# Sharing two-bank PSUM tiles between block products in the last group's first layer

## The chip, the cores and the metric

The kernel runs on one core of a Trainium2 chip. The metric is the device time in microseconds of one launch; the kernel before took 513.73 us (median of 3 runs, 512.77 to 514.19). A core has TensorE (PE, matrix products, written into PSUM), VectorE (DVE), ScalarE (ACT), GpSimd (POOL), and SyncE (SP), which issues DMAs. PSUM has eight banks; each holds 512 fp32 numbers in each of 128 partitions. The engines run their own instruction queues in order and wait for one another by semaphores.

## The reference

Two blocks follow each other. The first is a delta-rule attention over 4 batches, 8 heads, 768 tokens and a head dimension of 48:

```
k_n = k / (norm(k) + 1e-6)
for t in range(S):
    y[t] = q[t] @ state
    v_old = state^T k_n[t]
    state += beta[t] * outer(k_n[t], v[t] - v_old)
```

The result is laid out as x with 3072 rows (tokens) of 384 columns, and goes through a feed-forward block whose hidden layer is the maximum of three products:

```
h = max(x @ w1, x @ w2, x @ w3)      # w1, w2, w3: 384 x 768
out = h @ w_out                      # 768 x 384
```

## The kernel before, in words

The tokens are worked in six groups of 512. The attention of later groups is interleaved with the feed-forward part (`ffn`, a generator) of earlier ones, in an order written out by hand; a framework records which instruction writes and reads each tile and places the semaphore waits. When the last group's feed-forward part starts there is no attention work left, so from there to the end the kernel is one chain of layers.

From the second group on, the first product is taken out of the maximum: the kernel holds the differences w2-w1 and w3-w1 and computes h = max(0, x(w2-w1), x(w3-w1)), and x·w1·w_out is added in the output layer. In the code the differences are `w_sb[1]` and `w_sb[2]`.

For the last group the hidden layer is `crossed_hidden` (L1067). It splits the tokens into two halves of 256 (`lo`, `hi`) and the 768 hidden columns into two halves of three blocks of 128, and forms the four blocks of such a 2x2 product from seven products of sums and differences in place of eight. That covers the first two of x's three row blocks of 128; the third is added directly (`c1`, `c2`). A *unit* is one block pair j (three of them) and one difference matrix i (two), six in all. A unit makes eight block products, numbered 0 to 7, each 128 x 256 in fp32, with 1, 2, 1, 1, 1, 2, 2 and 1 matmuls (L1102), so 11 a unit:

- products 0, 2, 3 and 4 are copied to SBUF by ScalarE (L1121, L1127, L1130, L1134) as m1, m7, m5, m6;
- after product 4 VectorE adds these up in four steps (L1135 to L1138);
- products 1, 5, 6 and 7 are each read by VectorE (L1108), which adds them to a base in SBUF; in units with i = 1 a second VectorE instruction (L1110) takes the maximum with the hidden value of i = 0.

Four sums of the input halves (s1 to s4, L1083 to L1086) are made by VectorE ahead of the first unit.

A product's place in PSUM comes from `bank(n)` (L1114). Two rings exist for the whole kernel and fill the eight banks: `ps_ffn` (L80), one-bank tiles in 2 buffers, and `ps_two` (L83), two-bank tiles in 3 buffers. In the kernel before, even products take the first bank of a `ps_two` tile, whose second bank stays unused, and odd ones a `ps_ffn` tile. A buffer that is handed out again is written only once the readers of its previous content are done.

After the six units `outputs` (L947) runs the last layer, also as a 2x2 product, with two `ps_ffn` tiles p and q (L955) that its matmuls (L960) fill by turns. The same function runs for the group before, directly ahead of `crossed_hidden`; its last store is issued in part by ScalarE's queue (L1043, L981).

Of the kernel before, what the change touches and what calls it, by code (L numbers as in the profile page):

```python
# [23 lines left out]
def kernel(  # L24
# [42 lines left out]
    TOK = 512  # L67
# [12 lines left out]
    def ps_ffn(shape, name):  # L80
        return psum.tile(shape, FP32, name=name, tag="ffn", bufs=2)

    def ps_two(name):  # L83
        return psum.tile([128, 2, 512], FP32, name=name, tag="two", bufs=3)
# [222 lines left out]
    def square(name):  # L307
        return work.tile([128, H, C], FP32, name=name, tag="square", bufs=17)
# [758 lines left out]
    def crossed_hidden(m, hs):  # L1067


        xt, vec = xts[m], nc.vector.tensor_tensor  # L1070
        plus = vec if m == GROUPS - 1 else nc.gpsimd.tensor_tensor
        lo, hi = slice(0, 256), slice(256, 512)
        a11, a12, a13 = (xt[:, t, lo] for t in range(KT))
        a21, a22, a23 = (xt[:, t, hi] for t in range(KT))
        spare = [t.rearrange("p a h d -> p (a h d)") for t in kmore]
        s1, s2, s3, s4 = (spare[0][:, 256 * n : 256 * (n + 1)] for n in range(4))
        parts = [
            work.tile([128, 2, HB * BL + HB], FP32, name=name, bufs=1).rearrange(
                "p s r -> p (s r)"
            )  # L1080
            for name in ("x_bl", "y_bl")
        ]
        vec(out=s3, in0=a11, in1=a21, op=ALU.subtract)  # L1083
        vec(out=s1, in0=a21, in1=a22, op=ALU.add)
        vec(out=s2, in0=s1, in1=a11, op=ALU.subtract)
        vec(out=s4, in0=a12, in1=s2, op=ALU.subtract)  # L1086
        for j in range(FT):
            hs[j] = square("h").rearrange("p h c -> p (h c)")
        for unit in range(2 * PAIRS):
            j, i = divmod(unit, 2)  # L1090
            w = {
                name: t[:, 128 * j : 128 * (j + 1)]
                for name, t in thirds[1 + i].items()
            }
            top, bottom = hs[j], hs[j + PAIRS]
            held = parts[unit % 2]
            m1, m5, m6, m7 = (held[:, 256 * n : 256 * (n + 1)] for n in range(4))
            c11 = spare[1][:, 256 * (unit // 2 % 2) :][:, 0:256]

            def times(to, *terms):  # L1100
                for n, (stays, moves) in enumerate(terms):
                    nc.tensor.matmul(  # L1102
                        to, w[stays], moves, start=(n == 0), stop=(n == len(terms) - 1)
                    )

            def result(h, base, p, spare=None):
                to = h if i == 0 else base if spare is None else spare
                vec(out=to, in0=base, in1=p, op=ALU.add)  # L1108
                if i:
                    nc.vector.scalar_tensor_tensor(  # L1110
                        out=h, in0=h, scalar=0.0, in1=to, op0=ALU.max, op1=ALU.max
                    )

            def bank(n):  # L1114
                return (ps_ffn([128, TOK], "p_e") if n % 2 else ps_two("p_c")[:, 0])[
                    :, 0:256
                ]

            p = bank(0)
            times(p, ("b11", a11))  # L1120
            nc.scalar.copy(m1, p)  # L1121
            p = bank(1)
            times(p, ("b21", a12), ("c1", a13))
            result(top[:, lo], m1, p, c11)
            p = bank(2)
            times(p, ("t3", s3))
            nc.scalar.copy(m7, p)  # L1127
            p = bank(3)
            times(p, ("t1", s1))
            nc.scalar.copy(m5, p)  # L1130
            yield
            p = bank(4)
            times(p, ("t2", s2))
            nc.scalar.copy(m6, p)  # L1134
            plus(out=m6, in0=m6, in1=m1, op=ALU.add)  # L1135
            plus(out=m1, in0=m6, in1=m5, op=ALU.add)
            plus(out=m7, in0=m7, in1=m6, op=ALU.add)
            plus(out=m5, in0=m5, in1=m7, op=ALU.add)  # L1138
            p = bank(5)
            times(p, ("c2", a13), ("b22", s4))  # L1140
            result(bottom[:, lo], m1, p)
            p = bank(6)
            times(p, ("t4", a22), ("c1", a23))
            result(top[:, hi], m7, p)
            p = bank(7)
            times(p, ("c2", a23))
            result(bottom[:, hi], m5, p)
            yield

    def ffn(m):  # L1150
# [32 lines left out]
        if m >= GROUPS - 1:  # L1183
            yield from crossed_hidden(m, hs)
            early = FT
# [288 lines left out]
```

## Time and profile before

| | |
|---|---|
| median of 3 runs | 513.73 us (512.77 to 514.19) |
| span of the profiled execution | 510.5 us |
| its own time | not taken apart; the median of the runs is 3.2 us over the span |
| PE busy | 491.1 us, 96% of the span |
| DVE, ACT, POOL busy | 349.9, 168.7, 192.7 us |
| first matmul of `crossed_hidden` | 454.06 us |
| first L960 matmul of the last output layer | 484.60 us |
| between them: PE busy, DVE busy, ACT busy | 30.16, 23.11, 8.94 us of 30.54 |

The profile is one execution of the program, with the start and length of every instruction. PE is the matmul side of TensorE and PEld its weight loads; an fp32 matmul of this kernel leaves two records on each. A matmul's record reaches from its start to the end of its results, so that records of successive matmuls overlap, and the distance between starts tells what one costs. "Idle before, releaser" is the time in which an engine did nothing ahead of an instruction, and what ended it. Times in views are microseconds from the start of the span, durations in lists with slashes are nanoseconds.

### The profile page before, as it was taken

The numbers are of one execution on the slowest core, as the hardware profiler recorded it, in microseconds if no ns is written. First come the engines' busy times: TensorE is split into PE (matmuls) and PEld (weight loads), VectorE is DVE, ScalarE is ACT, GpSimd is POOL, SyncE is SP. The second block draws the span as 40 slices with busy tenths as digits, with TensorE's granted clock in tenths as the row PEclk, the third lists the DMA queues.
The fourth block names the chain that finished last, engine by engine and source line by source line (L and its number), as shares of the span: only waits on it lengthen the run. The fifth ranks groups of instructions, "written<-read, shape, count | busy, mean of one in ns | idle before, by whom it ended". The sixth has DMA issues, their size and how long they took to land.

```text
span 510.5 us, 18528 instructions
## 1 busy us (share of the span) xinstructions
PE 491.1 (96%) x8016; PEld 333.1 (65%) x8016; DVE 349.9 (69%) x801; ACT 168.7 (33%) x320; POOL 192.7 (38%) x317
## 2 busy tenths in 40 slices
PE   7778989999999999999999999999999999999996
PEld 6567778756565565665555565555655556998796
DVE  5897799969996430899563987635897455456752
ACT  5585664884422242210252101252101412113210
POOL 7434372783491926670575770503130000000000
PEclk9755999999999999999999999999999999999999
DMA  8938869764055925353675454923343202230001
GB/s 111 192 64 221 194 151 155 195 199 100 5 148 140 175 46 130 99 143 83 144 136 130 120 137 94 174 37 92 80 116 81 44 3 64 54 71 2 0 17 46
DMA packets 106304, 53.49 MB, mean 105 GB/s; under 512 B 89712, under 2 KB 99984, under 8 KB 106224
## 3 DMA queue, kind: packets, MB, share of 16 engines
q1 hardware_dynamic: 94352, 31.35, 30.4%
q0 software_dynamic: 9472, 20.37, 16.4%
q8 instruction: 63, 1.03, 0.9%
q10 hardware_dynamic: 2400, 0.59, 0.6%
q14 instruction: 17, 0.14, 0.1%
HBM read 39.17 MB, written 13.11 MB: 102 GB/s over the span
## 4 chain that ended last, share of the span: by engine, by line
PE 73%; DVE 14%; DMA 5%; ACT 4%; SPq 2%; issue 2%; POOL 0%; DVEq 0%; ACTq 0%; POOLq 0%
PE p_h L1161 26%; PE p_o L1199 13%; PE p_o L960 9%; PE p_e L1102 3%; DVE tmp L552 3%; PE p_g L406 3%; PE p_c L1102 2%; PE p_m L894 2%; PE p_u L759 2%; DMA kmore<-in_k_dram 2%; PE p_k L731 2%; PE p_y L801 2%; DVE y_bl L556 2%; PE p_s L782 2%; PE p_j L714 1%
## 5 line engine op out<-in xcount | busy, mean ns | idle before, releaser
L1161 PE MATMUL p_h<-xt,w_sb 128*128 128x512 f32 (+1 forms) x450 | 187.5, 558 | 0.7 <-ACT xt L827 0.6
L1161 PEld LDWEIGHTS p_h<-xt,w_sb 128*128 128x128 f32 x450 | 82.3, 193 | 68.7 <-issue 61.8
L1199 PE MATMUL p_o<-wo_sb,h 128*128 128x384 f32 x192 | 65.3, 490 | 0.0
L1175 DVE TENSOR_TENSOR h<-h,p_h 128x512 f32<-128x512 f32 (+1 forms) x42 | 25.4, 606 | 53.9 <-PE p_h L1161 52.8
L552 DVE TENSOR_TENSOR tmp<-x_bl,y_bl 128x31 f32<-128x31 f32 (+20 forms) x139 | 51.3, 369 | 4.1
L556 DVE TENSOR_TENSOR y_bl<-y_bl,tmp 128x31 f32<-128x31 f32 (+20 forms) x139 | 48.5, 349 | 4.8
L1199 PEld LDWEIGHTS p_o<-wo_sb,h 128*128 128x128 f32 x192 | 35.7, 190 | 23.2
L364 POOL DMA_DIRECT2D turned<-in_q_dram x72 | 39.1, 551 | 4.3 <-POOL turned L359 2.9
L1205 ACT COPY o_sb<-p_o 128x384 f32<-128x384 f32 x16 | 7.7, 479 | 85.8 <-PE p_o L1199 79.8
L1171 ACT ACTIVATE h<-p_h 128x512 f32<-128x512 f32 x24 | 14.3, 597 | 63.4 <-PE p_h L1161 60.5
L254 POOL TENSOR_TENSOR w_sb<-mant,up 128x384 int32<-128x384 int32 x18 | 19.1, 1059 | 39.3 <-DVE mant L250 39.2
L406 PEld LDWEIGHTS p_g<-kqt 48*64 48x64 f32 x1216 | 24.6, 142 | 9.0 <-issue 6.4
L406 PE MATMUL p_g<-kqt 48*64 48x64 f32 (+1 forms) x1216 | 27.8, 242 | 0.9 <-ACT kqt L335 0.8
L789 DVE TENSOR_TENSOR st<-st,p_s 48x768 f32<-48x768 f32 (+1 forms) x18 | 17.1, 949 | 15.4 <-PE p_s L782 15.2
L120 POOL DMA_DIRECT2D kpad<-in_k_dram x32 | 21.8, 690 | 14.1 <-issue 12.7
L1199 PE MATMUL p_o<-w_sb,xt 128*128 128x384 f32 x72 | 25.2, 486 | 0.0
L139 POOL DMA_DIRECT2D v_t<-in_v_dram x14 | 11.5, 829 | 35.5 <-PE p_u L759 35.5
L390 DVE TENSOR_TENSOR pt<-p_g,mask 128x512 f32<-128x512 f32 x20 | 13.8, 688 | 15.9 <-PE p_g L406 15.8
L287 POOL TENSOR_TENSOR v_t<-v_t,nrm 128x768 f32<-128x768 f32 x12 | 17.9, 1493 | 9.0 <-DVE nrm L281 8.9
L359 POOL MEMSET turned<- 128x96 f32 x18 | 3.3, 192 | 47.6 <-DVE kqt L380 47.6
L759 PEld LDWEIGHTS p_u<-v_t,ut 64*64 64x64 f32 x768 | 13.4, 141 | 10.1 <-issue 7.8
L1199 PEld LDWEIGHTS p_o<-w_sb,xt 128*128 128x128 f32 x72 | 13.7, 190 | 9.5
(212 smaller groups left out, 837.0 us busy)
## 6 DMA issues: line engine op xcount, KB each, us to landing
out_dram<-o_sb SPq DMA_DIRECT2D x40, 96.0 KB
w_bits<-in_moe_w_dram SPq DMA_DIRECT2D x9, 384.0 KB
w_bits<-in_moe_w_dram POOLq DMA_DIRECT2D x9, 384.0 KB, 5.2
turned<-in_q_dram POOLq DMA_DIRECT2D x72, 48.0 KB, 2.9
kpad<-in_k_dram POOLq DMA_DIRECT2D x32, 96.0 KB, 6.1
y_x<-y SPq DMA_DIRECT2D x16, 192.0 KB
qall<-y_x SPq DMA_DIRECT2D x32, 96.0 KB
v_t<-in_v_dram POOLq DMA_DIRECT2D x14, 192.0 KB, 5.0
```

The lines of the kernel that those rows point to most:

```text
L120: queues[bb].dma_start(out=dst[rows(bb ^ g), :, 0:D], in_=src[2 * bb + g, :, c * C : (c + 1) * C, :].rearrange("h p d -> p h d"),)
L254: nc.gpsimd.tensor_tensor(out=dst.bitcast(I32), in0=mant_v.bitcast(I32), in1=up_v, op=ALU.add)
L364: (queue, nc.gpsimd)[i].dma_start(out=t[p0 : p0 + 32, bb, at : at + NP * 2 * D].rearrange("p (j x) -> p j x", j=NP), in_=(k, q)[i][2 * bb ...
L406: nc.tensor.matmul(p_g[rows(bb ^ (g * i)), par, c0 : c0 + C * (1 + whole)], kq[:, 0], kq if whole else kq[:, i],)
L552: nc.vector.tensor_tensor(out=t_v, in0=row.to_broadcast(t_v.shape), in1=column.to_broadcast(t_v.shape), op=ALU.mult,)
L556: nc.vector.tensor_tensor(out=rest, in0=rest, in1=t_v, op=ALU.subtract)
L759: nc.tensor.matmul(p_v[rows(bb ^ g), g, i], ut[c % NU][rows(bb), g, h], rhs[rows(bb), g, h],)
L960: nc.tensor.matmul(to[:, g], a[j][:, 128 * g : 128 * (g + 1)], b[j], start=(start and g == j == 0), stop=(stop and g == 1 and j == PAIRS - 1),
L1102: nc.tensor.matmul(to, w[stays], moves, start=(n == 0), stop=(n == len(terms) - 1))
L1161: nc.tensor.matmul(p_h, w_sb[i][:, t, f * 128 : (f + 1) * 128], xt[:, t, lo : lo + w], start=(t == 0), stop=(t == KT - 1),)
L1175: nc.vector.tensor_tensor(out=h, in0=h, in1=p_h, op=ALU.max)
L1199: nc.tensor.matmul(p_o, stays, moves, start=(n == 0), stop=(n == len(terms) - 1))
```

## The change

Products 0 to 5 now take the two banks of a `ps_two` tile by pairs: (0,1), (2,3), (4,5), the even one in the first bank and the odd one in the second. Products 6 and 7 take one `ps_ffn` tile each. A unit thus asks for three `ps_two` and two `ps_ffn` tiles where it asked for four and four. The matmuls, copies and sums and their order stay the same. From L1089 on the changed file's lines are one higher, and from L1116 four higher.

```diff
         for j in range(FT):
             hs[j] = square("h").rearrange("p h c -> p (h c)")
+        pair = [None]
         for unit in range(2 * PAIRS):
...
             def bank(n):
-                return (ps_ffn([128, TOK], "p_e") if n % 2 else ps_two("p_c")[:, 0])[
-                    :, 0:256
-                ]
+
+                if n > 5:
+                    return ps_ffn([128, TOK], "p_e")[:, 0:256]
+                if n % 2 == 0:
+                    pair[0] = ps_two("p_c")
+                return pair[0][:, n % 2, 0:256]
```

## The prediction

> **What bounds the kernel now.** I read the page first, for the engine that decides.
>
> ```profile
> span 510.5 us, 18528 instructions
> PE 491.1 (96%) x8016; PEld 333.1 (65%) x8016; DVE 349.9 (69%) x801; ACT 168.7 (33%) x320; POOL 192.7 (38%) x317
> PE   7778989999999999999999999999999999999996
> PEclk9755999999999999999999999999999999999999
> ```
>
> TensorE is busy 96% of the span, so what delays a matmul of the last group lengthens the kernel. Next the windows over the changed stage (first L1102 matmul to the first L960 matmul behind it) and over three early stretches. Columns: stretch, length, busy time and count of PE, PEld, DVE, ACT, POOL, granted clock, DMA share, GB/s.
>
> ```profile
> 12.06:15.48 3.42, 1.77 (x68) 1.46 (x68) 2.85 (x6) 2.07 (x6) 2.19 (x3) 1.00 0.98 169
> 22.30:25.72 3.42, 1.96 (x56) 1.51 (x59) 3.04 (x12) 1.80 (x4) 0.00 (x0) 1.00 1.33 185
> 63.26:66.68 3.42, 2.15 (x70) 1.64 (x69) 3.32 (x8) 2.13 (x5) 0.92 (x2) 1.00 0.37 102
> 454.06:484.60 30.54, 30.16 (x133) 24.23 (x132) 23.11 (x61) 8.94 (x24) 0.00 (x0) 1.00 0.05 14
> ```
>
> In the stage's 30.54 us PE is busy for 30.16 at full clock, ACT for only 8.94. The timeline of the stage gives the prices (start, length, engine, line; in brackets the idle time before and what ended it).
>
> ```profile
> 454.06 0.59 PE L1102 MATMUL p_c<-xt,w_sb 128*128 128x256 f32 x2
> 454.84 0.68 ACTq L981 DMA_DIRECT2D out_dram<-up  x1
> 455.56 0.37 ACT L1121 COPY x_bl<-p_c 128x256 f32<-128x256 f32 x1 [10.52 <-PE p_e L1102]
> 456.32 0.41 DVE L1108 TENSOR_TENSOR h<-x_bl,p_e 128x256 f32<-128x256 f32 x1
> 456.79 0.70 PE L1102 MATMUL p_e<-xt,w_sb 128*128 128x256 f32 x2
> ...
> 460.34 0.59 PE L1102 MATMUL p_c<-kmore,crossed 128*128 128x256 f32 x2
> 460.98 0.37 ACT L1127 COPY y_bl<-p_c 128x256 f32<-128x256 f32 x1 [0.92 <-PE p_c L1102]
> 461.21 0.59 PE L1102 MATMUL p_c<-kmore,crossed 128*128 128x256 f32 x2
> 463.80 0.59 PE L1102 MATMUL p_c<-xt,w_sb 128*128 128x256 f32 x2
> ```
>
> To be seen: one matmul leaves two records and takes 0.432 us of PE (461.21 to 463.80 is six of them, 2.59 us). Its results are there 0.59 us after its start, and ScalarE's copy begins 0.05 later (460.93 to 460.98). The copy lasts 0.37. The last view, from the end of the stage and from an early wait of PE on ScalarE:
>
> ```profile
> 482.14 0.37 ACT L1134 COPY y_bl<-p_c 128x256 f32<-128x256 f32 x1
> 484.60 0.43 PE L960 MATMUL p_o<-wo_sb,h 128*128 128x192 f32 x1 [0.34 <-DVE y_bl L1108]
> ```
>
> ```profile
> L335 ACT COPY kqt<-p_t x2: 586/588/591, 11.8 to 12.3; 128x512 f32<-128x512 f32 x2
> ```
>
> The first L335 copy starts at 11.79, ends at 12.38, and the matmul that waits for it starts at 12.43: 0.05 from the end of a ScalarE copy to PE.
>
> **The change part by part.** Matmuls, copies and VectorE's work keep their number and order; no DMA moves, and no queue (SP, POOL) is passed. What changes is which tile a product is written to, and so which waits stand on the matmuls.
>
> *Removed.* The stage's 66 matmuls (11 a unit) need 66 x 0.432 = 28.5 us, and it lasts 30.54. So 2.0 us are waits now: some 1.5 us on VectorE's readings of the two one-bank buffers within the stage (as the one behind 456.32) and about 0.5 at L960. After the change a product's place comes back a whole unit later, so the waits inside the units go.
>
> *Added.* The order of the built changed program, with its waits, shows the decisive thing: the first matmul of products 1, 3 and 5 of every unit waits for ScalarE, and the count it waits for is that of the copies L1121, L1127 and L1134 of the same unit. Those read the other half of the same pair. Writing the second bank of a tile is thus held until the first bank has been read; before, the two products lay in different tiles. That makes 18 waits. Each stops the whole PE queue, since TensorE takes its matmuls in order, and behind it stand the rest of the unit and the output layer.
>
> The price of one, on PE: 0.59 (even product to its end) + 0.05 (to the copy) + 0.37 (copy) + 0.05 (back to PE) = 1.06 instead of 0.432, so 0.63. After a wait the weights are loaded only then: the pair of records that waited at 456.79 is 0.70 long and not 0.59, so 0.11 more. I take 0.63 + 0.11 = 0.74. Lower bound 0.63 (the load hidden); upper 0.79 (one semaphore instruction of 0.05, as this stage's L1102 row of 51 ns, stands ahead). The value lies with the rows of the stage itself.
>
> *First wait.* ScalarE is busy issuing the last store of the group before (454.84 to 455.52), so the first copy starts at 455.56, as now; before, nobody on PE waited for it. It ends at 455.93, PE resumes at 455.98 and, with the 0.11, at 456.09 instead of 454.49: 1.60.
>
> *Last wait.* The first L960 matmul now reuses the buffer of product 6, freed by VectorE's L1108. In the last unit now VectorE's chain from the L1134 copy's end (482.51) has product 5 read at +2.04 (484.55) and product 6 at +2.83. After the change that copy ends 4.65 into the unit: the five matmuls of products 0 to 3 (2.16) and two waits of 0.74 put product 4's start at 3.64, plus 0.59 + 0.05 + 0.37. Product 6 is read at 7.48, PE resumes at 7.53; the unit's matmuls end at 11 x 0.432 + 3 x 0.74 = 6.97. So 0.56 is left.
>
> *Sum.* 28.5 + 17 x 0.74 + 1.60 + 0.56 = 43.2 us, against 30.54: **+12.7 us**. The output layer behind (484.60 to the end, 25.9 us) only moves: its VectorE inputs get 0.8 us more lead. Costed at nothing: VectorE's work, 23.11 us in a stage of 43; POOL has none there. The profiled execution has a span of 510.5; the median of the runs is 513.73, so 3.2 lie around it. Span 523.2, time 526.4.
>
> *A rule against it.* The row: 1.06 us from an even product's start to the odd one's, because of a wait that the program carries. The Trainium skill, "PSUM — Partial Sum Buffer", section "PSUM bank collisions raise a hardware error", says that two engines collide in one bank and quadrant, while different banks run clean; by it the odd product needs no wait at all, and the sum would be a gain of up to 2 us. No run here shows a collision. I go by the built program.
>
> *The clock.* In the trace it fell to half right behind the two stretches in which PE was busy 1.77 and 1.96 of 3.42 us (15.48 and 25.72), and stayed behind the one of 2.15. In the changed stage gaps of 0.47 us three times in 6.97 leave PE busy 80%, 2.7 of 3.42, above all three. Only the first wait (idle 454.65 to 455.98) with the next one can leave less than 2 us in such a stretch. The skill's page "TensorE: Matmul & The Clock Gate", section "Why this matters for your kernels", asks for idle gaps over some 3 us before the clock falls. The two early stretches have none over 1.5 us, so the trace is stricter; by the page the loss is 0, by the trace up to one half-clock stretch.
>
> **The rivals.**
> 1. *The change does what it says* (the other side): the odd products don't wait, eight products are in flight. Gain 2.0 - 0.5 (last wait stays) = 1.5, time 512.2. It speaks for it that the two halves are used apart; against it the waits named above. It decides if those counts are reached before PE comes there, that is if a copy could end within 0.432 us of its product's start; the rows need 1.01.
> 2. *Clock falls once:* the first wait and the next fall into one stretch. A unit at half clock takes 6.97 + 4.75 = 11.7, so a stretch of 3.41 us loses 1.4: 527.8. If it stayed half for the stage, 28.5 more: 555.
> 3. *Cheaper waits:* 0.63 apiece, 18 x 0.11 less: 524.4. *Dearer:* 0.79, 18 x 0.05 more: 527.3.
>
> **How the numbers follow.** Forecast (0.71 to 0.77 a wait) 0.70; cheaper 0.12, dearer 0.07, one clock stretch 0.06, half clock throughout 0.02, no waits 0.03. The run-to-run spread is 512.77 to 514.19, so no change can be told within 0.3%, 1.5 us. Cheap waits at the fast end of that spread (1.0 below its median) give 523.4; dear ones with one lost clock stretch and the slow end (0.5 above) 529.2. Faster 0.015 and same 0.015 share rival 1, whose gain lies at that border; slower 0.97.
>
> **What would show it.** L1102's matmuls stay at 132 records; 18 PE idle gaps of about 0.47 us ended by ScalarE at L1121, L1127, L1134 (their new lines); units of 7.0 us and a stage of 43; L960's wait on VectorE as now; everything before 454 unchanged. Wrong if PE's waits on ScalarE are absent, if the clock is below 1.00 in the stage, or if the stage before 454 moves.

## The result and the profile after

The changed kernel takes 525.03 us (median of 5 runs, 523.68 to 526.33), the kernel before, in 5 runs, 512.77 (512.18 to 514.19). The ratio is 1.0233, with a 95% interval of 1.0203 to 1.0264: slower by 12 us. The prediction was 526.4, range 523.4 to 529.2.

The page of the changed kernel (the profiled execution took 526.33 us, the slowest of its five, with 1.8 us around the span):

```profile
span 524.5 us, 18530 instructions
PE 493.4 (94%) x8016; PEld 331.3 (63%) x8016; DVE 351.2 (67%) x801; ACT 168.8 (32%) x320; POOL 192.8 (37%) x317
PE   7578989999999999999999999999999999977896
PEclk9855999999999999999999999999999999999999
```

PE's row now has a dent of three slices near the end (7, 7, 8), where it stood at 9 before; the clock has none. The windows over the stage, from the first L1103 matmul (L1102 before) to the first L960 matmul, in the columns used before:

```profile
455.45:498.50 43.05, 33.47 (x135) 23.41 (x133) 24.74 (x63) 8.94 (x24) 0.00 (x0) 1.00 0.04 10
```

43.05 us in place of 30.54, so 12.5 more; behind it to the end of the span it is 26.0 as before (25.9). PE idles for 9.6 us of it, 9.2 ahead of L1103 matmuls and 0.4 ahead of the first L960 one. What ended the idle time is in the view of the line L1103 (microseconds in total, times):

```profile
its engine sat idle before it (us, times) until:
  ACT x_bl L1125: 5.7, 6
  ACT x_bl L1138: 4.0, 6
  ACT y_bl L1138: 4.0, 6
  ACT x_bl L1131: 4.0, 6
  ACT y_bl L1125: 4.0, 6
  ACT y_bl L1131: 4.0, 6
```

L1125, L1131 and L1138 are the copies of products 0, 2 and 4 (L1121, L1127 and L1134 before), and nothing else is in the list. It counts PE's matmuls and weight loads apart, so each gap twice; on the matmul side there are 18 such gaps, one of 1.31 us and 17 of 0.46. Rows of PE and ScalarE from the timeline show the long first gap with the DMA that ScalarE's queue issues, one of the common gaps in the second unit, and the end of the stage:

```profile
456.24 0.65 ACTq L981 DMA_DIRECT2D out_dram<-up  x1
456.93 0.37 ACT L1125 COPY x_bl<-p_c 128x256 f32<-128x256 f32 x1 [10.49 <-DVE kmore L1084]
457.36 1.13 PE L1103 MATMUL p_c<-xt,w_sb 128*128 128x256 f32 x4 [1.31 <-ACT x_bl L1125]
...
463.24 0.59 PE L1103 MATMUL p_c<-xt,w_sb 128*128 128x256 f32 x2
463.87 0.37 ACT L1125 COPY y_bl<-p_c 128x256 f32<-128x256 f32 x1 [2.95 <-PE p_c L1103]
464.29 1.13 PE L1103 MATMUL p_c<-xt,w_sb 128*128 128x256 f32 x4 [0.46 <-ACT y_bl L1125]
470.17 0.59 PE L1103 MATMUL p_c<-xt,w_sb 128*128 128x256 f32 x2
...
498.50 1.73 PE L960 MATMUL p_o<-wo_sb,h 128*128 128x192 f32 x9 [0.41 <-DVE y_bl L1109]
```

In the second unit product 0 starts at 463.24 and is there at 463.83; the copy runs from 463.87 to 464.24; product 1, which goes into the next bank, starts at 464.29. From this product 0 to that of the next unit (470.17) it is 6.93 us.

### The profile page after: what moved, and what is told of

Its sections match the earlier page's. It is cut to its first block, busy times and chain, and to the rows that moved or that the text cites. A ratio compares the mean times of both kernels' runs of the same rounds, so it can differ in the third digit from the quotient of the medians.

```text
span 524.5 us, 18530 instructions
## 1 busy us (share of the span) xinstructions
PE 493.4 (94%) x8016; PEld 331.3 (63%) x8016; DVE 351.2 (67%) x801; ACT 168.8 (32%) x320; POOL 192.8 (37%) x317
## 4 chain that ended last, share of the span: by engine, by line
PE 76%; DVE 12%; ACT 5%; DMA 3%; issue 2%; SPq 2%; POOL 0%; DVEq 0%; ACTq 0%; POOLq 0%
PE p_h L1165 27%; PE p_o L1203 16%; PE p_o L960 8%; PE p_c L1103 5%; PE p_g L406 3%; PE p_m L894 2%; PE p_u L759 2%; DVE tmp L552 2%; PE p_k L731 2%; DMA kmore<-in_k_dram 2%; PE p_s L782 2%; PE p_y L801 2%; PE p_q L731 1%; PE p_j L714 1%; PE p_e L1103 1%
## 5 line engine op out<-in xcount | busy, mean ns | idle before, releaser
L120 POOL DMA_DIRECT2D kpad<-in_k_dram x32 | 21.8, 690 | 13.8 <-issue 12.7
L1103 PE MATMUL p_c<-xt,w_sb 128*128 128x256 f32 x48 | 14.5, 405 | 6.4 <-ACT x_bl L1125 2.2
```

The source lines that it names most:

```text
L120: queues[bb].dma_start(out=dst[rows(bb ^ g), :, 0:D], in_=src[2 * bb + g, :, c * C : (c + 1) * C, :].rearrange("h p d -> p h d"),)
L1103: nc.tensor.matmul(to, w[stays], moves, start=(n == 0), stop=(n == len(terms) - 1))
```

## The experiments

Two theories were set against each other. *The order theory:* a write into one half of a two-bank tile is held until the other half has been read, and the 12.5 us are these waits. *The layout theory:* two banks handed out as one tile, or a copy beside a write into the next bank, are dear by themselves. Stages run from the first matmul of the unit loop to the first L960 matmul of the last layer. Diffs are against the changed kernel. Two baselines matter for what follows: the stage is 30.54 us before and 43.05 as changed. Ratios are to the kernel before.

### The second halves written late

```diff
-        pair = [None]
+        pair = {}
...
-                if n > 5:
+                if n == 0 == unit:
+                    return ps_two("p_c")[:, 0, 0:256]
+                if n < 2:
                     return ps_ffn([128, TOK], "p_e")[:, 0:256]
-                if n % 2 == 0:
-                    pair[0] = ps_two("p_c")
-                return pair[0][:, n % 2, 0:256]
+                if n < 5:
+                    pair[n] = ps_two("p_c")
+                    return pair[n][:, 0, 0:256]
+                return pair[n - 3][:, 1, 0:256]
```

> Products 2, 3 and 4 open the two-bank tiles and 5, 6 and 7 take their second halves; 0 and 1 take the one-bank tiles (product 0 of the first unit takes a two-bank tile of its own). Tiles are still shared, but each second half is written three products after the first, when the first has long been read. Theory (a write to one half is held until the other half has been read): the matmuls that open a second half find the copy done, no PE waits on ScalarE, the stage takes the bare 66 x 0.432 = 28.5 us, 2.0 under the kernel before: 510.8 on a base of 512.8, ratio 0.996. Rival (sharing two banks of a tile is itself dear, whatever the order: the copy's read beside a write into the next bank): 18 products are still written into second halves, so the stage stays near 43 us and the ratio near 1.02.

Ratio 0.9931 (0.9904 to 0.9958), median 510.09 against 513.43. The windows over its stage:

```profile
454.57:483.14 28.57, 28.57 (x133) 24.85 (x133) 22.68 (x59) 8.95 (x24) 0.00 (x0) 1.00 0.06 15
```

PE is busy in all of the 28.57 us: no gap is left. Three products of a unit are still written into second halves, as in the changed kernel, and the stage is 14.5 us shorter. The layout theory falls. The stage's gain over before, 1.97 us, is what the theory said; the ratio asks for more, so the kernel ran again:

> The kernel of late_halves once more. Its stage was 28.58 us against 30.54 before, 1.96 less, but its ratio of 0.9931 asks for 3.5 us. Theory (the rest is the scatter of the part ahead of the stage, which starts at 452.6 to 457.6 in the profiles so far): ratio 0.996, stage 28.6 again. Rival (something outside the stage gains too): ratio 0.993 again.

Ratio 0.9930 (0.9904 to 0.9957), stage 28.58, as long as the first time. So the rival's number came, but no profile shows where the other 1.5 us are: behind the stage the profiles of both kernels show 25.8 to 25.9 us, and ahead of it nothing was changed. It stays open. Either way this kernel is the fastest of all here.

### Both products written, then both read

```diff
             p = bank(0)
             times(p, ("b11", a11))
+            r = bank(1)
+            times(r, ("b21", a12), ("c1", a13))
             nc.scalar.copy(m1, p)
-            p = bank(1)
-            times(p, ("b21", a12), ("c1", a13))
-            result(top[:, lo], m1, p, c11)
+            result(top[:, lo], m1, r, c11)
...
```

(and likewise for products 2 and 3, and 4 and 5)

> The changed kernel's pairs (0,1), (2,3), (4,5), but both products of a pair are written before either is read. Theory (the wait comes from the read standing between the two writes): no PE wait on ScalarE inside pairs; the stage is 28.5 us and the wait ahead of the output layer. If reads are held back by the tile's last write too, product 4's copy starts after product 5's end, 0.86 us later, and the L960 wait grows to some 2.2 us: 30.8, ratio 1.000 to 1.001. If reads look at their own half only: 29.9, ratio 0.999. Rival (the layout is dear): near 43 us, ratio near 1.02.

Ratio 0.9992 (0.9966 to 1.0018), stage 30.68 us: the first of the two sub-cases, 30.8. The end of the last unit in the timeline:

```profile
480.27 0.59 PE L1103 MATMUL p_c<-kmore,w_sb 128*128 128x256 f32 x2
480.90 0.38 ACT L1140 COPY y_bl<-p_c 128x256 f32<-128x256 f32 x1 [0.65 <-PE p_c L1103]
484.17 2.81 PE L960 MATMUL p_o<-wo_sb,h 128*128 128x192 f32 x11 [2.01 <-DVE y_bl L1109]
```

The pairs are the changed kernel's, and all 18 gaps are gone; what was dear is the read between the two writes. The wait works in the other direction too: the copy of product 4 starts at 480.90, 0.04 us behind the last matmul of product 5 (480.86), though product 4 was done earlier. The later copy delays VectorE's sums, and PE's one remaining gap is 2.01 us ahead of the last layer. Behind the stage the profiled execution took 27.6 us in place of 25.9, since the clock fell there for a while (last section); the ratio doesn't show these 1.7 us, and whether the other executions had them no trace tells.

### Eight one-bank tiles

(the diff is shortened)

```diff
+    rings = ctx.enter_context(ExitStack())
+    pools = [rings.enter_context(tc.tile_pool(name="psum", ...))]
...
     def ps_ffn(shape, name):
+        if len(pools) > 1:
+            return pools[1].tile(shape, FP32, name=name, tag="one", bufs=8)
...
             def bank(n):
+                return ps_ffn([128, TOK], "p_e")[:, 0:256]
...
         if m >= GROUPS - 1:
+            rings.close()
+            pools.append(rings.enter_context(tc.tile_pool(name="last", ...)))
             yield from crossed_hidden(m, hs)
```

> For the last group the two rings are given up for one ring of eight one-bank tiles; no tile is shared, and a product's place comes back eight products later, as the change has it. Theory: what the change could have brought without shared tiles. No waits inside the units, none ahead of the output layer, but the first matmul waits for the last reader of the old rings (454.81 in the profile before, so 0.9 us lost): 29.4 us, 1.1 under before, ratio 0.998. Rival (the eight-product distance is of no use): ratio 1.000.

Ratio 0.9980 (0.9957 to 1.0002), as expected for the theory, though the interval does not quite shut out no change. The profile is clearer: 28.59 us from the first matmul with no gap, after the one wait that was expected at the entry:

```profile
457.00 0.56 DVE L994 TENSOR_TENSOR up<-up,p_o 128x384 f32<-128x384 f32 x1 [1.40 <-PE p_o L965]
457.61 1.56 PE L1108 MATMUL p_e<-xt,w_sb 128*128 128x256 f32 x6 [0.65 <-DVE up L994]
```

This is what the change could bring with its reuse distance of eight products and without shared tiles: about 2 us (30.54 against 28.59), of which this form gives 0.8 back at the entry: 0.65 of idle time, and the 0.16 by which a matmul's record otherwise overlaps the one before. That makes the 29.4 us expected.

### Half of the units

```diff
             def bank(n):

+                if unit > 2:
+                    return (ps_ffn([128, TOK], "p_e") if n % 2 else ps_two("p_c")[:, 0])[
+                        :, 0:256
+                    ]
                 if n > 5:
```

> Units 0 to 2 as changed, units 3 to 5 as before. Theory: the loss goes with the number of waits. 7.8 + 2 x 7.0 for the first three units, 15.6 for the last three as in the profile before: 37.4 us, 6.9 over before, ratio 1.013, nine PE waits on ScalarE. Rival (the loss is made at the entry or exit of the stage): ratio 1.023 or 1.000.

The windows over its two halves:

```profile
452.64:474.30 21.66, 16.65 (x68) 11.80 (x67) 12.60 (x32) 4.47 (x12) 0.00 (x0) 1.00 0.08 20
474.30:489.72 15.42, 15.05 (x68) 12.09 (x66) 11.09 (x30) 4.48 (x12) 0.00 (x0) 1.00 0.01 1
```

21.66 us for the units as changed (expected 21.8) and 15.42 for those as before (15.6), with nine waits on ScalarE. The ratio was 1.0088 (1.0054 to 1.0122), less than the stage's 6.5 us ask for. The same kernel ran again:

> The kernel of half_units once more. Its stage was 37.08 us, 6.54 over before, its ratio 1.0088 asks for 4.5. Theory (scatter ahead of the stage): ratio 1.0127, stage 37.1. Rival: 1.009 again.

Ratio 1.0132 (1.0098 to 1.0166), stage 37.07. The loss goes with the number of waits. The two ratios differ by 0.44% at equal stages: the part ahead of the stage scatters (it ended at 452.64 in one of the two profiles and at 453.91 in the other), and a ratio alone can't tell 2 us here.

### Each copy made twice

```diff
             nc.scalar.copy(m1, p)
+            nc.scalar.copy(m1, p)
...
             nc.scalar.copy(m7, p)
+            nc.scalar.copy(m7, p)
...
             nc.scalar.copy(m6, p)
+            nc.scalar.copy(m6, p)
```

> The changed kernel with the copies of products 0, 2 and 4 (m1, m7, m6) made twice, same source and target; the result is the same. Theory (the wait lasts from the even product's end to the end of the last read of its half): each of the 18 waits is longer by one copy and its start, 0.43 us as in the row of two copies following each other; 18 x 0.43 = 7.7 us more than the changed kernel, stage 50.8, ratio to before 1.038. Rival (the price is on PE, in reloading weights or in writing a neighbour bank, and ScalarE has slack: 8.9 us busy of 43): ratio stays at 1.023 to 1.025.

Ratio 1.0449 (1.0416 to 1.0483), median 535.47 against 512.97, stage 51.65. One wait in its timeline:

```profile
458.22 0.59 PE L1103 MATMUL p_c<-kmore,crossed 128*128 128x256 f32 x2
458.85 0.37 ACT L1132 COPY x_bl<-p_c 128x256 f32<-128x256 f32 x1 [1.65 <-PE p_c L1103]
459.25 0.37 ACT L1133 COPY x_bl<-p_c 128x256 f32<-128x256 f32 x1
459.68 1.13 PE L1103 MATMUL p_c<-kmore,crossed 128*128 128x256 f32 x4 [0.86 <-ACT x_bl L1133]
```

The gap grew from 0.46 to 0.86 us: each wait lasts as long as the reads of the other half do, though ScalarE is mostly idle. A steady unit, with three gaps, takes 8.15 us in place of 6.94, 1.21 more; six of them make 7.3 us, where 7.7 were expected. The stage grew by 8.6; the other 1.3 us are in the last unit, where the clock fell (last section). The ratio lies above the 1.038 that the theory gave: the medians differ by 22.5 us, the stages by 21.1, and where the last 1.4 us are no profile shows.

### The store ahead of the stage on SP's queue

```diff
-        store(m5, 1, 1, both_queues)
+        store(m5, 1, 1, both_queues if m == GROUPS - 1 else one_queue)
```

> The changed kernel with the last store of the group before issued wholly by SP's queue, so that ScalarE's queue isn't busy issuing a DMA when the first product is ready. Theory: the first wait falls from 1.59 to the common 0.73, the stage from 43.05 to 42.2, ratio to before 1.0216 against 1.0233; other waits unchanged. Rival (the first copy waits for something else): first wait unchanged.

```profile
455.75 0.59 PE L1103 MATMUL p_c<-xt,w_sb 128*128 128x256 f32 x2
456.38 0.37 ACT L1125 COPY x_bl<-p_c 128x256 f32<-128x256 f32 x1 [9.66 <-PE p_c L1103]
456.81 1.13 PE L1103 MATMUL p_c<-xt,w_sb 128*128 128x256 f32 x4 [0.46 <-ACT x_bl L1125]
```

The first copy now follows its product at once, the first gap is 0.46 like all others, and the stage is 42.19 us, 0.86 less. So the longer first wait was the DMA that ScalarE's queue was issuing. The ratio, 1.0243 (1.0207 to 1.0278), can't resolve 0.86 us.

### Other pairs: (0,3), (1,4), (2,5)

```diff
-        pair = [None]
+        pair = {}
...
-                if n % 2 == 0:
-                    pair[0] = ps_two("p_c")
-                return pair[0][:, n % 2, 0:256]
+                if n < 3:
+                    pair[n] = ps_two("p_c")
+                return pair[n % 3][:, n // 3, 0:256]
```

> The changed kernel with pairs (0,3), (1,4), (2,5) in place of (0,1), (2,3), (4,5); 6 and 7 in the one-bank tiles as changed. Theory (a write into one half is held until the other half has been read, so what counts is when that read ends): 3 and 5 find the copies of 0 and 2 done; 4 waits for VectorE's read of product 1, which in units 2 and 4 comes only after VectorE's last sums of the unit before, 2.8 us into the unit in the profile before, against 2.16 for product 4: 0.83 with the weight load, twice. The L960 wait is on product 6's read, 1.4. Stage 28.5 + 1.7 + 1.4 = 31.6, ratio 1.002, no PE wait on ScalarE. Rival (any two products between the two writes are enough): 29.9, ratio 0.999.

Ratio 1.0024 (0.9999 to 1.0048), stage 32.15 us against 31.6 expected. In its third unit:

```profile
467.63 0.70 PE L1103 MATMUL p_c<-kmore,crossed 128*128 128x256 f32 x2 [0.57 <-DVE h L1109]
```

The matmul held here is product 4, and it waits for VectorE's read of product 1, in units 2 and 4, as the theory said; those units take 5.58 us against 4.75 bare (0.84 more each, expected 0.83). The wait ahead of the last layer is 1.3 us (1.4 expected). Missed was the first unit, 5.42 us, where the late first copy reaches product 3 and, through product 1's sum, product 4. Distance in the order of products is not what counts; the end of the other half's read is.

## Why the prediction was right

**The mechanism** was read from the waits of the built program, not from the diff, which says that two banks are used apart. Late second halves, reads after both writes, and one-bank tiles each removed all 18 gaps, by three different ways; doubling the copies lengthened each by one copy.

**The price of a wait**, 0.74, was measured as 0.73: a steady unit takes 6.94 us, 4.75 of matmuls and three waits. Its parts hold singly: 0.59 to the product's end, 0.04 to the copy, 0.37 copy, 0.05 back, and 0.11 for the weight load that starts only then (a waiting pair of records is 0.70 long). The prediction's lower bound of 0.63, with the load hidden, is excluded.

**The first wait**, 1.60, was 1.58, and the run with the store on SP's queue shows its cause. **The last wait**, 0.56, was 0.58 (the last unit takes 7.51 us up to L960, a steady one 6.94). **The sum**, 43.2 us, was 43.05; 12.7 more was 12.5. The time was 1.4 us under the forecast although the sum missed by 0.2: 1.0 of it is the base, the median of three runs, 513.73, where five gave 512.77. The 3.2 us that the section on the time before and the prediction count around the span are only in part what an execution takes beyond its span: in every execution on record here that is 1.8 to 2.1 us. The rest is that the profiled execution of the kernel before was a fast one.

**A sign that was too sharp.** The prediction calls itself wrong if the part ahead of 454 moves, and the changed stage begins at 455.45, 1.4 us later than in the profile before. But two profiles of one and the same kernel begin it at 454.57 and 455.79 (the late halves), so a move of this size shows nothing.

**What was removed** was read rightly too: the 2.0 us of waits before are real, since a stage without any takes 28.57 to 28.59 us (28.5 from 66 x 0.432).

**The rivals.** That the change does what it says was right to be given little: it needs second halves that are not held, and only other kernels had that. The rule of the Trainium skill ("PSUM — Partial Sum Buffer", "PSUM bank collisions raise a hardware error"), by which different banks run clean, is not contradicted: the wait is one that the program carries, and the late halves, which write one bank while another is read, show no loss from it (28.57 us without a gap). Whether the chip would need these waits is not shown: no run takes the wait alone away and leaves the order as it is. The clock stayed at 1.00 in the changed stage, in the profiled execution. Its changes in this trace, at 17.05, 20.46, 27.29 and 54.60 us, lie whole multiples of 3.41 us apart, and the early stretches that the prediction judges by end on such steps of their own trace (15.48 and 25.72). In the changed kernel a step at 457.37 (54.60 and 118 times 3.413) parts the long first gap from the next one, and the stretch with the long gap was busy for 2.11 us:

```profile
453.95:457.37 3.42, 2.11 (x14) 1.71 (x12) 1.96 (x5) 0.37 (x1) 0.00 (x0) 1.00 0.51 115
```

So the rival's condition, less than 2 us, was not met in this execution, and where the step fell was luck. In the run with half of the units, which has the same first gap, the stretch took in that gap and a part of the next one. It was busy for 1.85 us, and the clock stayed all the same:

```profile
452.95:456.36 3.41, 1.85 (x8) 1.06 (x6) 2.39 (x6) 0.59 (x2) 0.00 (x0) 1.00 0.46 115
```

But that rival is real: the clock fell in two other kernels, as the last section shows.

## What to carry to other kernels

Ask of a tile that spans several banks which instruction reads it between two writes: where the framework orders accesses by tile, the second write waits for that read, and the price is a full round trip between engines less the work that the waiting engine can do meanwhile (here 0.73 us, 17 times, and once 1.58, on the engine that sets the end). Write all banks before the first read, write the second one when the first has long been read, or take one tile per bank; the number of products in flight alone says little. A built program's waits and a handful of rows of the old profile are enough to price this to a few per cent.

## What the runs showed that was not expected

*The clock falls without a long gap.* In the run with doubled copies, two stretches between such steps had the same busy PE (1.68 of 3.41 us, no gap over 0.87). Behind the second the clock was halved for 3.41 us, behind the first it was not. The windows (the clock is the third number from the right):

```profile
488.87:492.28 3.41, 1.68 (x8) 1.07 (x7) 1.62 (x5) 1.49 (x4) 0.00 (x0) 1.00 0.00 0
499.11:502.52 3.41, 1.68 (x8) 0.82 (x7) 0.98 (x3) 1.86 (x5) 0.00 (x0) 1.00 0.00 0
502.52:505.94 3.42, 3.42 (x9) 2.70 (x10) 2.32 (x6) 0.00 (x0) 0.00 (x0) 0.50 0.00 0
```

It explains the 1.3 us of that stage that the waits don't: matmuls there start 0.85 us apart (at 503.34 and 504.19) in place of 0.43, and the wait of 0.58 ahead of the last layer is gone in it. The kernel that reads after both writes had the same behind its gap of 2.01 us:

```profile
481.90:485.31 3.41, 1.40 (x9) 1.15 (x8) 3.27 (x10) 0.00 (x0) 0.00 (x0) 1.00 0.00 0
485.31:488.73 3.42, 3.42 (x13) 3.42 (x12) 2.06 (x7) 0.48 (x1) 0.00 (x0) 0.50 0.00 0
```

The Trainium skill's rule ("TensorE: Matmul & The Clock Gate", "Why this matters for your kernels"), that gaps over some 3 us are to be avoided, would have let all of these pass. Nor is the line of the prediction, about 2 us busy in a stretch, sharp: the clock stayed behind 1.68 and 1.85 here and fell behind 1.96 in the kernel before, and behind 2.21 in an early stretch of the kernel with eight one-bank tiles (104.08 to 107.49). The prediction's 1.5 us for the longest early gap counts what lies inside its stretches; the gap at the end of the first runs on, from 14.20 to 16.14. What else counts is open.

*The late halves gain 0.7%* in two measurements where their stage explains 0.4%. No run tells where the rest is.
